# Pair 3 of batch 0 turned by transposing transfers, centroid halves in two banks, wide tanh and gate in the first unit, and a new written order

## The chip, the cores and the metric

The kernel runs on one core of one Trainium2 chip. The metric is device time in microseconds, the median of several runs. The kernel before took 301.54 us (three runs, 300.48 to 303.38).

The core has five engines with a queue each, and they run side by side: PE multiplies matrices, DVE and ACT do elementwise work (ACT has exp and tanh), POOL does simple elementwise work, and SP issues transfers. An engine takes its instructions strictly in the order in which they were written. An instruction whose inputs are not ready holds up everything behind it on its engine.

## The reference, cut to what matters

Clustered attention for 4 batches, 8 heads, 768 positions and head size 64, and behind it a two-layer network over the 3072 tokens.

```python
q_assign = argmax(einsum('bhsd,hcd->bhsc', q / |q|, c / |c|))   # 16 centroids per head
k_assign = argmax(einsum('bhsd,hcd->bhsc', k / |k|, c / |c|))
mask     = q_assign[:, :, :, None] == k_assign[:, :, None, :]
scores   = where(mask, q @ k.T / 8, -1e9)
attn     = exp(scores - max) / sum(exp(scores - max))
x        = (attn @ v) as [3072, 512]
h        = x @ w_in                 # 512 -> 2048
out      = (h * sigmoid(h)) @ w_out # 2048 -> 512
```

The argmax has to be right for nearly every position, so the products with the centroids need more than 16 bits. The kernel splits q and k into a high and a low float16 part.

## The kernel before, in words

**Tiles.** A batch has 8 heads in 4 pairs (pair p holds heads 2p and 2p+1). A head has 6 tiles of 128 positions for k and 6 for q. Each pair has a buffer `ab` in SBUF in which every tile lies turned: 64 rows of the high part and, in rows 64 to 95, a one-hot code of the tile's cluster, scaled so that the product of two different codes drives the exponent to zero. Scores are then one product of 96 rows (L685), with the mask in it.

**Steps.** `build` makes a graph of steps, each with the engines that may do it. Names in this document are those tags. For a part of batch b, pair p, head h, from tile t they are `p{b}.{p}.{h}.{t}` with a letter:

- `t` turns the tiles, `hi` and `lo` make the two parts, `v` moves half of the high part to the lower rows
- `l` multiplies with the centroids (logits), `m`, `b`, `o`, `f` find the largest, subtract it, make the one-hot code and flip it in blocks of 32
- `c` puts the code into `ab`, four copies of 32 rows, each by POOL, DVE, ACT or as a transfer on SP

Attention steps are `a{b}.{head}.{first q tile}`: `S` scores (L685), `E` exp (L688), `V` product with v (L713), `R` and `N` reciprocal and normalisation, `X` the turn of the result (L770) and `Y` its copy. Units of the network are `m{b}.{first tile}`: `U` up (L801), `T` tanh (L809), `G` gate (L812), `D` down (L828), `L` copy out, `O` store. Loads are `ld{b}.{p}` (q, k) and `lv{b}.{p}` (v), `cv` the cast of v; `win`, `wout` load weights and `cin`, `cout` cast them.

**Two ways to turn a part.** `part2` (L562 on, used for the first 8 tiles of each head of batch 0: 6 of k, 2 of q) turns two float32 tiles at once on PE (L579, four transposes per head), makes `hi` and `lo` out of PSUM and then moves half of `hi` with `v`. Its logits are three products for each pair of tiles (L624 to L626), with centroids that lie in `st2`. For pairs marked "22" the two heads share one round of `m`, `b`, `o`, `f`; pair 0, marked "2", has one round for each head. `part` (L465 on) splits the tiles as they lie in SBUF and turns both parts together with one transposing transfer on SP (L517), and its logits are products with `stk` (L529, L530 in batch 0, L532 later). All other parts go this way: q tiles 2 to 5 of batch 0 (`p0.p.0.8`) and batches 1 to 3.

**Stages.** Batch 0 goes in three rounds of two q tiles ([0,2), [2,4), [4,6)) so that the first unit of the network, `m0.0` (tokens of q tiles 0 and 1, all 8 heads), can start early. `m0.0` has 256 columns. Its 16 `U` steps are 4 matmuls of 256 columns each, its 16 tanh and 16 gates are 256 wide. The other units are `m0.2` with 512 columns and two of 384 in each later batch.

**Order.** The order on every engine is written out by hand: `PLAN` is a packed list of (step, engine) in order and of buffer numbers. It also holds dummy products with zeros (L951), 43 of 256 columns, in places where PE would wait. There are 8 PSUM banks; each `S`, `U`, `D`, turn and logit step takes one.

**The centroids** (L307 to L361) are loaded on ACT's queue, normalised (`csq` on DVE, `croot` on POOL, `csplit` on DVE), turned by one transpose of [128 x 128] into one bank (`cturn`, L330), and copied: `cplace2` into `st2` (two steps of two copies, one on ACT, one on DVE), and `cplace` into `stk` (three copies on DVE).

Of the kernel before, what the change touches and what calls it, by code (L numbers as in the profile page):

```python
# [12 lines left out]
f32 = mybir.dt.float32  # L13
f16 = mybir.dt.float16
AF = mybir.ActivationFunctionType
ALU = mybir.AluOpType
# [9 lines left out]
    "11543XvaUa;<08X8W*vvspm({+9jHIiazwtnnkkNf5nk&?iyp>(J@a+%_i5zs8%TrcSts4^|Y{weeZ43*}M&!mD2no=3a?r4yn=N*jx(y&wjafjU"
    "2n;uFckmvp8&K5U|(Bnke-4Enr6k{oPB=#GuV_$L?p)?s33mRMbRk*w&duya{%9ll)m~1~F!Tyo^$=#F{*HO&)q#=*7O59YGrf@%A}!W>11<7t+|"
    "7hD_`@X7{wSAv4m;rJxy~Xe&*?+||p$h<Uc+E@<W*WAfg$^(Ee9jl=W8rs~AlxJb4!lW5*2Y<65#Bdx6_VY7Q)#JT3WsM&>(jlGD8&sg(s*UZ<;f"
    "{@u&=b=3b{Ld~%Y_C_jV{Dwbe)c(bH&W|()aGDnop<~^5BT*t*3Z@l8Jb$H!)8yy_IXiTQ<LoZkYM&M?2nDo<L!UMRP2DMJTd02bY<%E!)67&EOt"
    "zO25c4a)+lP{=o-~ZCfMp6XXmW=k1;Fe%`3@N)u4IPklBl{t%TmXI(|gQnf&y2FWzLeYi1iV@t<1rBmUF8=#84l4%=u?G^2uk74z~zRX3eoy@*+*"  # L30
# [957 lines left out]
```

## Time and profile before

| | |
|---|---|
| median of three runs | 301.54 us |
| the profiled execution's own time | 301.66 us |
| its span, first to last instruction | 299.9 us |
| granted TensorE clock | 0.998 |
| busy: PE, DVE, ACT, POOL | 291.2, 213.9, 222.6, 89.6 us |
| first scores, first exp | 12.22, 13.50 us |
| first `U` of the first unit, its first tanh | 38.7, 39.77 us |
| first `U` of the second unit | 59.9 us |
| last matmul starts | 296.6 us |

Times inside a run count from the span's start. The profiled execution's own time is 1.8 us longer than its span. Matmuls overlap, so their listed durations are longer than their share of PE; how fast PE goes is read from how far apart their starts lie.

### The profile page before, as it was taken

What the parts mean: (1) busy time and instruction counts of PE and PEld (TensorE: products, weight loads), DVE (VectorE), ACT (ScalarE), POOL (GpSimd) and SP (SyncE); (2) the same over time, 40 slices, a digit from 0 to 9 for tenths busy, and PEclk for the clock granted to TensorE, in tenths of its full rate; (3) what the DMA queues carried; (4) which work ended last, traced back from release to release, by engine and by line L of the source; (5) the groups of instructions that cost most, each with busy time, mean ns of one, the idle gap of its engine ahead of it and who ended that gap; (6) DMA issues with size and microseconds to landing.
All of it is one profiled execution on the core that took longest, in us unless ns stands there. A gap on an engine that the chain in (4) does not pass through costs nothing.

```text
span 299.9 us, 7820 instructions
## 1 busy us (share of the span) xinstructions
PE 291.2 (97%) x3044; PEld 187.0 (62%) x3044; DVE 213.9 (71%) x512; ACT 222.6 (74%) x456; POOL 89.6 (30%) x151
## 2 busy tenths in 40 slices
PE   7898999999999999999999999999999999999995
PEld 5776898645555676766656566566665655554553
DVE  5999988878898999889999686676552323465140
ACT  2898999888669898998888867889988732343221
POOL 3787776443655406040833212100200000000000
PEclk9999999999999999999999999999999999999999
DMA  7899999498999999899485688500201111021022
GB/s 203 263 227 291 218 262 348 116 281 293 249 283 243 232 245 215 224 202 300 124 170 126 134 144 196 149 5 3 66 2 26 28 32 67 0 93 49 1 107 105
DMA packets 83382, 47.42 MB, mean 158 GB/s; under 512 B 60688, under 2 KB 78352, under 8 KB 83344
## 3 DMA queue, kind: packets, MB, share of 16 engines
q1 hardware_dynamic: 83200, 46.88, 63.6%
q8 instruction: 24, 0.39, 0.6%
q14 instruction: 14, 0.11, 0.1%
q10 hardware_dynamic: 144, 0.03, 0.1%
HBM read 27.30 MB, written 6.29 MB: 112 GB/s over the span
## 4 chain that ended last, share of the span: by engine, by line
PE 83%; DVE 10%; ACT 2%; issue 2%; DMA 1%; POOL 1%; SPq 0%; DVEq 0%
PE M L801 26%; PE M L828 26%; PE M L685 17%; PE M L713 10%; DVE hl L459 3%; PE M L532 2%; DMA nat<-in_q_dram 1%; DVE gq L812 1%; DVE lo L599 1%; DVE ab L191 1%; DVE ohT L436 1%; POOL ab L191 1%; DVE oh L429 1%; DVE mx L419 1%; DVE M L422 1%
## 5 line engine op out<-in xcount | busy, mean ns | idle before, releaser
L688 ACT ACTIVATE P<-M 128x512 f16<-128x512 f32 x288 | 155.8, 622 | 18.6 <-PE M L685 17.9
L812 DVE SCALAR_TENSOR_TENSOR gq<-tn,M 128x384 f16<-128x384 f32 (+2 forms) x128 | 66.7, 548 | 47.9 <-ACT tn L809 46.4
L801 PE MATMUL M<-xt,win_s 128*128 128x384 f16 (+2 forms) x512 | 95.7, 325 | 0.0
L828 PE MATMUL M<-wout_s,gq 128*128 128x512 f16 (+2 forms) x400 | 94.8, 370 | 0.0
L685 PE MATMUL M<-ab 96*128 96x256 f16 (+1 forms) x432 | 90.5, 308 | 1.4 <-DVE ab L191 0.9
L809 ACT ACTIVATE tn<-M 128x384 f32<-128x384 f32 (+2 forms) x128 | 61.2, 512 | 36.5 <-PE M L801 32.4
L801 PEld LDWEIGHTS <-win_s 128*128 128x128 f16 x512 | 48.7, 97 | 33.5 <-issue 0.2
L828 PEld LDWEIGHTS <-gq 128*128 128x128 f16 x400 | 37.4, 97 | 36.2 <-issue 0.4
L191 POOL COPY ab<-ohT 32x384 f16<-32x384 f16 (+2 forms) x69 | 38.4, 557 | 55.6 <-DVE ohT L436 31.2
L713 PEld LDWEIGHTS <-P 128*128 128x128 f16 x1152 | 45.7, 97 | 10.5 <-issue 0.7
L713 PE MATMUL M<-vt,P 128*128 128x65 f16 x1152 | 49.2, 193 | 0.3 <-DVE oh L429 0.2
L685 PEld LDWEIGHTS <-ab 96*128 96x128 f16 x432 | 38.0, 97 | 18.3 <-DVE ab L191 0.7
L459 DVE SCALAR_TENSOR_TENSOR hl<-nat,hl 128x768 f16<-128x768 f32 (+1 forms) x28 | 29.6, 1073 | 0.1
L191 POOL CAST vt<-nv 128x384 f16<-128x384 f32 x19 | 11.3, 607 | 32.5 <-DMA nv<-in_v_dram 21.3
L456 POOL TENSOR_SCALAR hl<-nat 128x768 f16<-128x768 f32 (+1 forms) x19 | 15.1, 804 | 19.4 <-DMA nat<-in_k_dram 14.2
L436 DVE STREAM_TRANSPOSE ohT<-oh 128x384 f16<-128x384 f16 (+2 forms) x33 | 18.3, 557 | 1.0
L401 DVE TENSOR_REDUCE M<-M 128x192 f32<-128x384 f32 x24 | 13.4, 559 | 6.1 <-PE M L532 4.4
L189 ACT COPY ot<-M 128x512 f32<-128x512 f32 (+2 forms) x14 | 7.8, 558 | 12.0 <-PE M L828 12.0
L191 DVE COPY ot<-M 128x512 f32<-128x512 f32 x11 | 7.6, 687 | 8.9 <-PE M L828 8.9
L429 DVE TENSOR_SCALAR oh<-M 128x96 f16<-128x96 f32 (+4 forms) x62 | 13.1, 252 | 0.7
L743 DVE TENSOR_TENSOR xn<-M,rz 128x384 f16<-128x384 f32 x24 | 13.1, 551 | 0.7 <-DVE rz L732 0.3
L732 DVE RECIPROCAL rz<-M 128x6 f32<-128x6 f32 (+1 forms) x36 | 6.6, 182 | 8.3 <-PE M L713 8.1
(60 smaller groups left out, 174.6 us busy)
## 6 DMA issues: line engine op xcount, KB each, us to landing
nv<-in_v_dram SPq DMA_DIRECT2D x16, 384.0 KB, 5.1
out_dram<-ot SPq DMA_DIRECT2D x23, 256.0 KB, 2.5
nat<-in_k_dram SPq DMA_DIRECT2D x15, 384.0 KB, 4.7
...
```

Source lines behind the costliest of these rows:

```text
L191: eng(en).tensor_copy(out, in_)
L429: e.nc.vector.tensor_scalar(out=T(oh)[:, 0:n, 0:HC].rearrange("p (g i) c -> p g i c", g=groups)[:, :, i0:i1, :], in0=from_().rearrange("p ...
L436: e.nc.vector.transpose(T(ohT)[:, 0:n, :].rearrange("p n c -> p (n c)"), T(oh)[:, 0:n, :].rearrange("p n c -> p (n c)"))
L456: e.nc.gpsimd.tensor_scalar(out=dh(), in0=src(), scalar1=QS, scalar2=1.0, op0=ALU.mult, op1=ALU.mult)
L459: e.nc.vector.scalar_tensor_tensor(out=dl(), in0=src(), scalar=QS, in1=dh(), op0=ALU.mult, op1=ALU.subtract)
L685: e.nc.tensor.matmul(bank(sb)[:, at : at + 128 * (c - a)], ab[0:96, kt[m], :], q, start=True, stop=True)
L688: e.nc.scalar.activation(out=T(P)[:, 0:n], in_=bank(sb)[:, 0:n], func=AF.Exp, bias=0.0, scale=ESC)
L713: e.nc.tensor.matmul(bank(O)[:, at : at + D + 1], T(P)[:, c : c + 128], T(vb)[:, VW * m : VW * m + D + 1], start=(m == 0), stop=(m == NJ - ...
L801: e.nc.tensor.matmul(bank(bk)[:, 0:n], e.win_s[:, r, ts(fb, 128)], T(X)[:, r, 128 * j0 : 128 * j1], start=(r == 0), stop=(r == NR - 1),)
L809: e.nc.scalar.activation(out=T(tn)[:, 0:n], in_=bank(bk)[:, 0:n], func=AF.Tanh, bias=0.0, scale=1.0)
L812: e.nc.vector.scalar_tensor_tensor(out=gq(fb // 4)[:, fb % 4, 0:n], in0=T(tn)[:, 0:n], scalar=1.0, in1=bank(bk)[:, 0:n], op0=ALU.add, op1= ...
L828: e.nc.tensor.matmul(bank(bk)[:, 0 : c1 - c0], gq(quarter)[:, fc % 4, ts(t, 128)], e.wout_s[:, fc, c0:c1], start=(fc == 0), stop=(fc == NF ...
```

## The change

1. **Pair 3 of batch 0.** `FIRST` for pair 3 goes from "22" to "DMA": its first 8 tiles of each head go through `part`. Two steps `hi`, two steps `lo` of 8 tiles read SBUF, two transposing transfers turn them, logits are 16 tiles x 2 products with `stk`, and each head has its own `m`, `b`, `o`, `f`. The four `v` and `t` steps of this pair and its `lo2` are gone.
2. **Centroids.** The two halves are turned by two transposes into two banks. `cplace2` now copies heads 0 and 1 alone (two small copies per half), `cplace3` the other six heads. Pair 0's logits wait for `cplace2`, pairs 1 and 2 for `cplace3`. `cplace` waits for both.
3. **The first unit.** With n = 256 columns, two `U` steps share a bank, and one tanh and one gate of 512 columns serve both: 8 of each in place of 16. `D` steps wait for the wide gates. Units of 384 and 512 columns are as before.
4. **Sizes.** 21 buffers `P` for 19; `mx`, `oh`, `ohT` hold 16 tiles in place of 24; `half` is placed earlier; `EARLY` (empty) is gone.
5. **The order** is new on every engine, with 57 dummy products in place of 43.

```diff
-FIRST = ["2", "22", "22", "22"]
+FIRST = ["2","22","22","DMA"]
...
-    "P": (19, [128, 512], f16),
+    "P": (21, [128, 512], f16),
...
-    pc = buf("M", 64)
+    pcs = [buf("M", 64), buf("M", 64)]
...
-        e.nc.tensor.transpose(bank16(pc)[:, 0:128], e.chl.rearrange("p a d -> p (a d)"), e.ident)
+        for part, pc in enumerate(pcs):
+            e.nc.tensor.transpose(bank16(pc)[0:64, 0:128], e.chl[:, part, :], e.ident)
...
+    s_pair = [
+        step("DVE ACT", c_place2(part, 0, 2), after=[s, s_const2], use=[pcs[part]], kind="place2", size=300, tag="cplace2")
+        for part in range(2)
     ]
-    s_cent = step("DVE", c_place, after=[s, s_const, s_cent2], use=[pc], kind="const", size=690, tag="cplace")
+    s_others = [
+        step("DVE ACT", c_place2(part, 2, H), after=[s, s_pair[part]], use=[pcs[part]], kind="place2", size=430, tag="cplace3")
+        for part in range(2)
+    ]
+    s_cent = step("DVE", c_place, after=[s, s_const, s_others], use=pcs, kind="const", size=690, tag="cplace")
...
-        s_log = step("PE", logits, after=[s_hi, s_lo, s_cent2], use=[A, lo2, Lb], kind="mm", size=(3 * w, 32), tag=tag + "l", key=key + 1)
+        s_log = step("PE", logits, after=[s_hi, s_lo, s_others if p else s_pair], use=[A, lo2, Lb], kind="mm", size=(3 * w, 32), tag=tag + "l", key=key + 1)
...
+        per = 512 // n if n <= 256 else 1
+        for f0 in range(0, NFB, per):
+            bk, tn = buf("M", n * per), buf("tn")
...
+            for fb in range(f0, f0 + per):
...
+                ups.append(
+                    step("PE", up, after=[xs, w_done["in"][fb // 2], ups], use=[bk, X], kind="mm", size=(NR, n), tag=tag + "U", key=key + fb)
+                )
...
+            y = step("ACT", tanh, after=ups, use=[bk, tn], kind="T", size=n * per, tag=tag + "T", key=key + f0)
+            s = step("DVE", gate, after=[ups, y], use=[bk, tn, g4], kind="G", size=n * per, tag=tag + "G", key=key + f0)
+            gates.extend([s] * per)
```

The first steps of the order, read out of the packed list ("24 x" is a count of dummies; a number behind # tells repeated steps of one name apart; of a pair's loads, #0 is k, #1 the first two q tiles, the last one q tiles 2 to 5, and for pair 0 k comes in two, #0 for head 0 and #2 for head 1, with q at #1 and #3):

```
SP before   ld0.0#0 ld0.0#1 ld0.0#3 ld0.0#2 ld0.3#1 ld0.3#0 ld0.2#2 ld0.1#0 ld0.1#1 p0.0.0.8t ld0.2#1 ld0.2#0 lv0.3 lv0.0 ld0.1#2 p0.2.0.8t
SP after    ld0.3#1 ld0.3#0 ld0.0#1 ld0.0#0 ld0.0#3 ld0.0#2 lv0.3 ld0.1#1 p0.3.1.0t ld0.2#2 p0.3.0.0t ld0.1#0 ld0.2#1 p0.0.0.8t ld0.2#0 ld0.1#2

PE before   14x p0.0.0.0t 2x cturn 3x p0.0.1.0t 2x p0.0.0.0l 3x p0.3.1.0t p0.0.1.0l p0.3.0.0t 8x p0.1.1.0t p0.1.0.0t p0.0.0.8l a0.0.0S
PE after    24x p0.0.0.0t cturn 6x p0.0.1.0t p0.0.0.0l 8x p0.0.1.0l 9x a0.0.0S a0.0.0S a0.0.0S p0.3.0.0l p0.3.1.0l 2x p0.1.0.0t p0.1.1.0t a0.1.0S

ACT before  p0.0.0.0hi cplace2 p0.0.1.0hi p0.3.1.0hi p0.3.0.0hi c c c c p0.1.1.0hi p0.1.0.0hi E E E E p0.2.0.0hi p0.2.1.0hi E ...
ACT after   p0.3.1.0hi p0.0.0.0hi cplace2 cplace2 p0.0.1.0hi cplace3 cv0.3 p0.0.1.0v cplace3 c c E E E c p0.1.0.0hi p0.1.1.0hi E p0.1.1.0v E E p0.2.1.0hi E E p0.2.0.0hi E ...

DVE before  csplit p0.0.0.8hi cplace2 p0.0.0.0lo p0.0.0.8lo p0.0.0.0m p0.0.1.0lo b o (p0.0.1.0: m b) f ...
DVE after   csplit p0.3.1.0lo p0.3.0.0lo p0.0.0.8hi p0.0.0.0lo p0.0.0.8lo p0.0.0.0m b p0.0.1.0lo o f ...
```

Ahead of the first tanh ACT has 49 exps before and 50 after; ahead of the first `U` PE has 51 `S` steps, 12 `V`, 6 `X`, 12 logit steps and 8 turns before, and 50, 14, 5, 12 and 6 after.

More of the change, by code (lines that the diff above doesn't have):

```diff
@@ L26 @@
[L26 to L30, printed above, removed]
@@ L91 @@
 PAIRED = 6
-EARLY = {}
 CHUNK = 8
@@ L106 @@
     "xn": (3, [128, 6, 128], f16),
-    "mx": (3, [128, 24], f32),
-    "oh": (2, [128, 24, 32], f16),
-    "ohT": (2, [128, 24, 32], f16),
+    "mx": (3, [128, 16], f32),
+    "oh": (2, [128, 16, 32], f16),
+    "ohT": (2, [128, 16, 32], f16),
     "tn": (3, [128, 512], f32),
@@ L355, in build @@
     s = step("POOL", c_root, after=[s, s_ident], kind="const", size=520, tag="croot")
-    s = step("DVE", c_split, after=[s], kind="const", size=870, tag="csplit")
-    s = step("PE", c_turn, after=[s, s_ident], use=[pc], kind="mm", size=(1, 128), tag="cturn")
-    s_cent2 = [
-        step("DVE ACT", c_place2(part), after=[s, s_const2], use=[pc], kind="place2", size=2, tag="cplace2") for part in range(2)
-    ]
-    s_cent = step("DVE", c_place, after=[s, s_const, s_cent2], use=[pc], kind="const", size=690, tag="cplace")
+    s = step("DVE", c_split, after=[s], kind="const", size=950, tag="csplit")
+    s = step("PE", c_turn, after=[s, s_ident], use=pcs, kind="mm", size=(2, 128), tag="cturn")
+    s_pair = [
+        step("DVE ACT", c_place2(part, 0, 2), after=[s, s_const2], use=[pcs[part]], kind="place2", size=300, tag="cplace2")
+        for part in range(2)
+    ]
+    s_others = [
[3 more added lines that the diff above has]
+    s_cent = step("DVE", c_place, after=[s, s_const, s_others], use=pcs, kind="const", size=690, tag="cplace")
     abuf, ready = {}, {}
@@ L801, in up @@
                         e.nc.tensor.matmul(
[L802 to L806 removed]
+                            bank(bk)[:, c0 : c0 + n], e.win_s[:, r, ts(fb, 128)], T(X)[:, r, 128 * j0 : 128 * j1],
@@ L812, in gate @@
+            def gate(_, f0=f0, bk=bk, tn=tn):
                 e.nc.vector.scalar_tensor_tensor(
-                    out=gq(fb // 4)[:, fb % 4, 0:n], in0=T(tn)[:, 0:n], scalar=1.0, in1=bank(bk)[:, 0:n],
-                    op0=ALU.add, op1=ALU.mult,
-                )
-            y = step("ACT", tanh, after=[s], use=[bk, tn], kind="T", size=n, tag=tag + "T", key=key + fb)
-            gates.append(step("DVE", gate, after=[s, y], use=[bk, tn, g4], kind="G", size=n, tag=tag + "G", key=key + fb))
+                    out=gq(f0 // 4)[:, f0 % 4 : f0 % 4 + per, 0:n], in0=T(tn)[:, 0 : n * per].rearrange("p (f c) -> p f c", c=n),
+                    scalar=1.0, in1=bank(bk)[:, 0 : n * per].rearrange("p (f c) -> p f c", c=n), op0=ALU.add, op1=ALU.mult,
+                )
@@ L926 @@
     e.wout_s = const.tile([128, NFB, DM], f16, name="wout_s")
+    e.half = const.tile([128, 1], f32, name="half")
     e.ident = const.tile([128, 128], f16, name="ident")
```

144 lines of the change are left out of this document (68 added, 76 removed).

## The prediction

> **What bounds the kernel now.** I read the page's busy times first, then busy time in four stretches, the chain of waits, and then the engines' own time lines up to 40 us.
>
> ```profile
> span 299.9 us, 7820 instructions
> PE 291.2 (97%) x3044; PEld 187.0 (62%) x3044; DVE 213.9 (71%) x512; ACT 222.6 (74%) x456; POOL 89.6 (30%) x151
> ```
> ```profile
> 0.00:12.20 12.20, 10.17 (x97) 8.07 (x98) 8.54 (x31) 5.50 (x11) 5.08 (x26) 1.00 0.75 209
> 12.20:38.60 26.40, 23.65 (x414) 20.37 (x412) 25.45 (x71) 25.28 (x52) 20.95 (x35) 1.00 1.07 259
> 38.60:59.90 21.30, 20.73 (x294) 17.40 (x292) 17.90 (x51) 20.46 (x49) 13.80 (x18) 1.00 0.87 237
> 59.90:296.60 236.70, 236.47 (x2248) 141.14 (x2246) 161.98 (x362) 170.88 (x346) 49.75 (x74) 1.00 0.57 137
> ```
> ```profile
> 38.74 1.36 PE M L801 x12
> ...
> 41.27 0.73 PE M L713 x24
> ...
> 45.19 0.66 PE M L685 x6
> ```
>
> The second number of the stretches is their length, then come busy PE, weight loads, DVE, ACT, POOL. From 38.60 on PE is busy 257.2 of 258.0 us. So the end is set by two things: when PE becomes dense, and how much PE work is then left. The chain shows 38.74 as the start of the first `U`. Nothing after that can be won but some 0.8 us of idle PE and work taken off PE itself. From 12.2 to 38.6 it is different: ACT is busy 25.28 and DVE 25.45 of 26.40, PE 23.65 with dummies in it. There the exps on ACT and the codes on DVE meter the work out to PE. So for the change I ask how far PE has come in its work when the units of the network begin.
>
> **The change part by part.**
>
> *PE's own work.*
>
> ```profile
> 7.92 0.18 PE L624 MATMUL M<-st,ab 128*128 128x32 f16 x1
> ...
> 7.95 0.18 PE L625 MATMUL M<-st,ab 128*128 128x32 f16 x1
> ...
> 10.90 1.04 PE L579 MATMUL M<-ident,nat 128*128 128x128 f32 x8
> ```
>
> Eight float32 turns of pair 3 go: eight took 1.04 us to the end of the last, which I put at 0.11 each from start to start, 0.87. Small products start 0.03 apart (7.92, 7.95; a little under, since both are rounded): 24 go and 32 come, +0.2, and one more centroid turn, +0.07. Together PE has 0.6 us less to do. The dummies lie where PE would wait, before and after, so I take 14 more at nothing; the cover is the wait itself, and if a wait behind a dummy were gone, the ten small ones after the first scores would cost 0.11 each, 1.1 us, which is within the range.
>
> *The first scores.*
>
> ```profile
> 1.05 3.17 PE L951 MATMUL M<-zeros 128*128 128x256 f16 x14 [1.05 <-DVE zeros L196]
> ...
> 4.02 1.06 PE L579 MATMUL M<-ident,nat 128*128 128x128 f32 x4
> ```
> ```profile
> DMA packets 830, 0.65 MB, mean 130 GB/s; under 512 B 188, under 2 KB 830, under 8 KB 830
> ```
> ```profile
> DMA packets 288, 0.40 MB, mean 333 GB/s; under 512 B 13, under 2 KB 288, under 8 KB 288
> ```
> ```profile
> 5.14 0.28 DVE L323 SCALAR_TENSOR_TENSOR chl<-tn,ci,chl 128x64 f16<-128x64 f32 x1
> 5.90 0.84 DVE L454 TENSOR_SCALAR hl<-nat 128x512 f16<-128x512 f32 x1 [0.48 <-DMA nat<-in_q_dram]
> ...
> 7.13 0.69 DVE L599 SCALAR_TENSOR_TENSOR lo<-M,ab 128x512 f16<-128x512 f32 x1
> 7.74 0.68 DVE L459 SCALAR_TENSOR_TENSOR hl<-nat,hl 128x512 f16<-128x512 f32 x1
> 8.35 0.29 DVE L419 TENSOR_REDUCE mx<-M 128x8 f32<-128x128 f32 x1
> ...
> 10.29 0.43 DVE L436 STREAM_TRANSPOSE ohT<-oh 128x256 f16<-128x256 f16 x1
> ```
> ```profile
> 10.85 1.65 ACT L189 COPY ab<-ohT 32x256 f16<-32x256 f16 x4
> 12.53 1.08 ACT L594 ACTIVATE ab<-M 128x512 f16<-128x512 f32 x2
> 13.50 2.09 ACT L688 ACTIVATE P<-M 128x512 f16<-128x512 f32 x4
> 15.47 1.09 ACT L594 ACTIVATE ab<-M 128x512 f16<-128x512 f32 x2
> 16.43 12.04 ACT L688 ACTIVATE P<-M 128x512 f16<-128x512 f32 x24
> 29.30 3.54 ACT L688 ACTIVATE P<-M 128x512 f16<-128x512 f32 x7 [0.83 <-PE M L685]
> 33.09 6.96 ACT L688 ACTIVATE P<-M 128x512 f16<-128x512 f32 x14 [0.25 <-PE M L685]
> 39.77 0.55 ACT L809 ACTIVATE tn<-M 128x256 f32<-128x256 f32 x1
> 40.04 0.78 ACT L688 ACTIVATE P<-M 128x512 f16<-128x512 f32 x1
> ```
>
> The loads of pair 3 (0.13 + 0.39 MB) now stand ahead of pair 0's. Pair 0's first k and q end after 0.85 MB in place of 0.33. In the first 5 us 0.65 MB had moved (the first of the two packet rows, window 0 to 5 us); later the queue gives 0.40 MB in 1.2 us (the second, 12.4 to 13.6). So they land near 5.6 us, and the first turn starts there and not at 4.02. The 24 dummies fill this: 14 took 3.17 us, 0.22 each, so at that pace they'd end at 6.3, and at 5.6 if they speed up at 5 us as the turns do (four in 1.06 at 4.02, eight in 1.04 at 10.90).
>
> The lateness is hidden by DVE. After `csplit` (5.14 + 0.28) DVE now has two `lo` of pair 3, 0.6 each by the distance of 7.13 and 7.74, then p0.0.0.8hi (0.84, or less without its wait), and starts p0.0.0.0lo near 7.5 to 7.8, where it was 7.13. From there the order on DVE is nearly as before (8.35 is the first peak, 10.29 the flip): with one `lo` earlier in between I get the flip at 10.3 to 10.7. Two puts each on POOL and ACT follow, 0.41 apiece by the ACT row, where ACT had three in a row; scores at 11.8 to 12.1 for 12.22. The two `cplace2` on ACT (0.5 apiece at most) end near 7.9, in time for that `lo`. Then the gain: before, two `hi` of pair 1 stood ahead of the first exp (12.53, exp at 13.50). Now the exp comes first, 0.45 behind its scores: 12.25, that is 1.25 earlier.
>
> *ACT up to the first tanh.* Among the exps now stand one exp more (0.49), two `hi` more (0.97 by 12.53 to 13.50), one put (0.41) and p0.1.1.0v, a copy of [64 x 512].
>
> ```profile
> L191 POOL COPY ab<-ab 64x512 f16<-64x512 f16 x8 | 5.7, 727 | 3.6 <-ACT ab L594 3.4
> ```
>
> This copy ACT has not done before; it lies between its put of 256 columns, 0.41, and POOL's 0.73 for the same copy. I take 0.55. Sum +2.4 - 1.25 = +1.2. Idle ACT was 0.83 + 0.25 in this stretch, and I leave it at 1.1 to 1.2: it comes in other places, below. So the first tanh moves from 39.8 to 41.0 by ACT.
>
> DVE as a second count, from the first flip to the last copy of round [0,2): three `hi` come to DVE (+1.7 by 0.84 for one of 512 and less for the others), two `lo` have gone ahead of it (-1.2), codes of pair 3 go by head (+0.6), the codes of head 1 fall behind the flip (+0.6), three wide puts and one copy less (-1.3): +0.4. Between +0.4 and +1.2 I take +0.85, nearer to ACT, whose rows cover more of it.
>
> *The queue of SP.* Behind p0.3.1.0t and p0.3.0.0t, which wait for their `lo` (6.1 and 6.7), stand ld0.2#2, ld0.1#0, ld0.2#1, p0.0.0.8t and ld0.2#0. Pair 1's turns on PE wait for ld0.1#0, and with them ACT's two `hi` and every exp behind them.
>
> ```profile
> DMA packets 1091, 0.28 MB, mean 165 GB/s; under 512 B 1056, under 2 KB 1091, under 8 KB 1091
> ...
> ab<-hl SPq DMA_TRANSPOSE x1, 3.2
> ```
>
> The one transfer of this size (8 tiles, 0.26 MB; window 9.6 to 11.3) ran at 165 GB/s, 1.6 us of the queue, and landed 3.2 us after its issue. The loads ahead are 1.84 MB: at 333 GB/s from 5 us on they end at 8.6. Two such transfers (3.2), ld0.2#2 (0.8) and ld0.1#0 (1.2) then end at 13.8, usable near 14.1. ACT wants its first `hi` of pair 1 after three exps and a put, at 14.1 too, and the turn lies between: 0.5 us of idle ACT. For pair 2, ld0.2#0 ends at 17.0, and the same count leaves 0.2. With 0.5 for a late put later on that is the 1.2 of above.
> [...]
>
> *The wide tanh and gate.*
>
> ```profile
> L809 ACT ACTIVATE tn<-M 128x512 f32<-128x512 f32 x16 | 9.1, 600 | 4.3 <-PE M L801 3.4 <-DVE gq L812 0.5 <-ACT P L688 0.3
> ```
>
> A tanh of 256 holds ACT 0.27 (39.77 to 40.04). One of 512 lasts 0.60, and the exps of 512 follow each other at 0.50 (12.04 for 24). Eight at 0.50 for sixteen at 0.27 save 0.3 us; the gates save some of DVE's time, which isn't full there. Between 38.6 and 59.9 PE lacks 0.57, and ACT is the full one (20.46 of 21.30), so I credit 0.3.
> [...]
>
> *The rest.* The larger `P` pool and the smaller tiles cost nothing, and no row shows `S` waiting for a `P`. The order after 60 us is new too: PE is idle for 0.23 there now, so it can hardly gain, and I take 0, with 1 us of loss as its other end. The tail is the same: two narrow pieces, a copy, a store.
>
> *Sum.* The `U` steps begin 0.85 later; PE has then done 0.25 us less (one `S` of 0.22, one `X` and two turns of 0.44 less, two `V` of 0.37 and 0.2 of logits more), and has 0.6 less in all, so 0.35 less to do: +0.85 - 0.35 - 0.3 = +0.2. The profiled execution took 301.66, so 301.9; the median of the runs stands 0.1 below it: 301.7.
>
> **The rivals.**
>
> *PE dense from 20 us on (faster).* Pair 3's exps are at hand before pair 1's codes, and could fill the gaps that PE has today.
>
> ```profile
> 24.59 0.60 PE L685 MATMUL M<-ab 96*128 96x256 f16 x4 [0.27 <-DVE ab L191]
> ...
> 28.65 1.05 PE L685 MATMUL M<-ab 96*128 96x256 f16 x8 [0.64 <-DVE ab L191]
> ```
>
> For it: these gaps wait for DVE's puts of pairs 1 and 2, idle PE from 12.2 to 38.6 is 2.75 us, and the 11 dummies that the order has there (0.11 each, 1.2 us) hide more. Were nearly all of it gone, with the rest of the sum: 301.7 - 3.5 = 298.2. Against it: ACT and DVE are full in that stretch, and both get more to do.
>
> *SP's queue late (slower).* If each transposing transfer holds the queue until it lands, 3.2 us in place of 1.6, ld0.1#0 comes at 17.3, ACT and PE stand behind p0.1.0.0t, and the end moves by that: 301.7 + 3.2 = 304.9. It decides from 14.1 on: each us by which pair 1's k is later costs one. For it: the one such transfer started at an idle queue, so how it runs behind loads isn't shown. Against it: loads issued behind it moved data right after it.
>
> *Transfers as fast as loads.* At 333 GB/s each of the two takes 0.8, so the loads come 1.6 earlier and ACT's 0.7 of waiting for them goes: 301.0. The 165 GB/s speak against it. [...]
>
> *The change doesn't do what it says:* the wide tanh serves only 256-column units, so it can do no more than the 0.3; this is in the forecast.
>
> **How the numbers follow.** A change of under 1%, 3 us, can't be told from none; the three runs before spread by 2.9. Forecast 0.55, transfers as loads 0.07, dense PE 0.18, SP late 0.20. Faster by over 1%: 0.18 (298.2 is 1.1% below). Slower by over 1%: 0.20. Same: 0.62. Range: down to 298.0, where the dense rival lies, and up to 305.0, which takes in the slow one and the unknown late order.
>
> **What would show it.** Right: the first exp near 12.3, the first tanh near 41, the first `U` near 39.5, PE busy in all but 1 us from there, and DMA transposes at about 165 GB/s. Pair 1's turns at 14 to 15 us show the queue; at 17 the slow rival holds. PE idle under 1 us between 13 and 38 would be the dense rival. Wrong in any case if the distance from the first `U` to the last matmul isn't 257 to 259 us.

## The result, and the profile after

The changed kernel took 305.49 us (median of six runs), the kernel before 301.72 us beside it. The ratio is 1.0103, with a 95% interval of 1.0068 to 1.0137: the change is slower, and whether by more than the 1% that parts the prediction's classes can't be told. Two of the six runs (309.77 and 310.98) were in a slower state and don't count in the ratio; the other four have a median of 304.96. The prediction was 301.7 us, with a range of 298.0 to 305.0, so that median lies at its upper edge. The profiled execution took 305.32 us.

The page after (busy time), and then the busy time in the stretches that the prediction used: length, PE, weight loads, DVE, ACT, POOL, granted clock, DMA share, GB/s.

```profile
span 303.5 us, 7878 instructions
PE 292.9 (96%) x3059; PEld 188.0 (62%) x3059; DVE 206.7 (68%) x496; ACT 230.7 (76%) x466; POOL 83.0 (27%) x148
```
```profile
0.00:12.20 12.20, 9.45 (x81) 7.08 (x81) 7.99 (x27) 6.35 (x16) 4.57 (x25) 1.00 0.93 218
12.20:38.60 26.40, 23.81 (x407) 20.65 (x408) 23.27 (x69) 23.26 (x48) 18.06 (x33) 0.94 1.05 249
38.60:59.90 21.30, 21.30 (x318) 18.44 (x317) 17.25 (x47) 21.23 (x44) 13.90 (x19) 1.00 0.98 261
59.90:300.00 240.10, 237.98 (x2255) 141.61 (x2253) 157.86 (x354) 179.44 (x361) 46.46 (x71) 1.00 0.57 136
```

Two rows are worse than before. In the first, PE is less busy than it was (10.17). In the last it lacks 2.12 us, where it lacked 0.23. From 38.6 to 59.9 it is full now, where it lacked 0.57: the dense stretch comes as the prediction had it, and is worth about that much.

The lines of the engines' time line for the milestones (start, length, engine, line, what it does; in brackets the wait before it):

```profile
5.48 0.30 PE L581 MATMUL M<-ident,nat 128*128 128x128 f32 x1
6.79 0.55 PE L581 MATMUL M<-ident,nat 128*128 128x128 f32 x3 [1.01 <-DMA nat<-in_k_dram]
...
12.71 1.08 ACT L690 ACTIVATE P<-M 128x512 f16<-128x512 f32 x2 [0.56 <-PE M L687]
...
13.96 0.27 PE L581 MATMUL M<-ident,nat 128*128 128x128 f32 x1
...
41.45 0.60 PE L803 MATMUL M<-xt,win_s 128*128 128x256 f16 x4
```

These are the first product of pair 0's turn, on its q tiles (4.02 before), its other three, on k, the first exp (13.50 before), the first product of pair 1's turn, on q as well, and the first `U` (38.74 in the chain of before, 38.63 on PE's own line). Pair 1's k followed at 14.64. The first tanh started at 42.97 (39.77 before). The waits of PE from 5 to 25 us, of ACT from 12 to 41, and of PE from 100 to 122 (engine, line, releaser: us in all, how often, the longest):

```profile
PE M L531 <- DMA ab<-hl: 1.5, 1, 1.5
PE M L581 <- DMA nat<-in_k_dram: 1.4, 2, 1.0
...
ACT P L690 <- PE M L687: 1.6, 2, 1.0
ACT ab L596 <- PE M L581: 1.6, 3, 0.7
...
PE M L687 <- DVE M L403: 2.1, 1, 2.1
```

**The start.** L531 is p0.0.0.8l, the logits of pair 0's later q tiles. It waits for its transposing transfer, and everything behind it on PE waits too. The chain of waits has that transfer at 11.77 with 5.65 us to landing; the same transfer in the kernel before took 3.2.

```profile
11.77 5.65 DMA ab<-hl
17.43 0.05 issue
17.48 0.18 PE M L531
```

Why it took so long is seen in the transfers from 13.9 to 17.4 us (GB/s in 40 slices, and the one packet of PE's own instructions in that stretch):

```profile
GB/s 281 307 328 304 290 281 249 401 219 164 105 249 266 266 281 97 18 3 0 0 0 0 3 9 6 9 9 12 9 9 9 53 402 357 369 474 351 88 140 369
...
q8 instruction: 1, 0.02, 2.5%
```

For 1.3 us, from 15.3 to 16.6, the core's DMA engines moved next to nothing (6 GB/s in the mean); such a stretch is called a standstill below. A packet with 16 KB of PE's instructions was on its way from 14.52 to 15.92, and the 256-byte packets of the transposing transfer, of which half take 0.018 us or less, took up to 1.48.

**The clock.** Behind that wait the granted clock (the third number from the right) fell:

```profile
16.00:18.00 2.00, 0.53 (x17) 0.52 (x18) 0.89 (x2) 1.28 (x3) 1.69 (x5) 1.00 0.76 227
18.00:20.00 2.00, 2.00 (x25) 1.77 (x22) 1.83 (x5) 1.31 (x3) 0.00 (x0) 0.59 1.07 363
20.00:22.00 2.00, 2.00 (x22) 1.76 (x21) 1.77 (x5) 1.35 (x3) 1.70 (x4) 0.55 1.21 318
```

From 18.4 to 21.8 us the clock was at half (0.50 over these 3.4 us). Twelve large products and a dummy ran there at half pace, 0.213 apart for 0.108, some 0.105 us more each, 1.4 us in all; the small ones kept their distance of 0.027. PE was busy for 1.9 of the 3.4 us ahead of the fall, and for 1.3 of the 3.4 us from 115.25 on, where no fall followed, so an idle PE alone didn't decide it. Of the experiments' profiles that are read below only e11_start_only shows such a fall, and that at 94 us, so it isn't in every execution.

**The middle.** The other 2.1 us lie at 116 us. The engines' time line from 114 on (SPq is SP issuing a transfer):

```profile
112.78 1.48 SPq L519 DMA_TRANSPOSE ab<-hl  x1
...
115.47 2.10 SPq L762 DMA_TRANSPOSE xt<-xn  x1
...
117.47 0.56 DVE L456 TENSOR_SCALAR hl<-nat 128x768 f16<-128x768 f32 x1 [2.90 <-DMA nat<-in_q_dram]
117.94 0.56 DVE L403 TENSOR_REDUCE M<-M 128x192 f32<-128x384 f32 x1
```

DVE stands 2.9 us at p2.3.1.0hi, for the load ld2.3#1. Behind it stands the sum L403 that frees a PSUM bank, and PE wants that bank. The load was issued at 112.10, 2.5 us before DVE came to that step; in the kernel before SP issued it at 98.97, and DVE came to the step at 108.29. And again 16 KB of PE's instructions came (115.47), and the longest packet of the transposing transfer took 2.13 us.

**A ledger for PE.** For every matmul I take the distance to the next one's start, less the usual distance of its kind (the tenth percentile of its shape); dummies count whole. The sum is what PE didn't spend on the kernel's own work at its usual pace, in us by stretch:

| | 0-15 | 15-20 | 20-60 | 60-100 | 100-150 | behind | sum | last matmul ends |
|---|---|---|---|---|---|---|---|---|
| before | 8.28 | 1.40 | 5.58 | 1.00 | 0.76 | 1.32 | 18.34 | 296.80 |
| after | 10.47 | 2.61 | 4.48 | 0.63 | 2.92 | 1.77 | 22.86 | 300.35 |

The rest is the kernel's own work: 278.5 before, 277.5 after. So the end moved by 4.5 - 1.0 = +3.5: 2.2 were lost up to 15 us, 1.2 up to 20, 2.2 from 100 to 150 and 0.4 behind, and 1.1 + 0.4 were won between 20 and 100. Counted again with kinds told apart by the printed shapes, the sums come out within 0.25 us and the work saved at 0.6, so differences of 0.4 us in this ledger mean little.

### The profile page after: what moved, and what is told of

Same layout as the page of the kernel before. It is cut to its first block, busy times and chain, and to the rows that moved or that the text cites. A ratio compares the mean times of both kernels' runs of the same rounds, so it can differ in the third digit from the quotient of the medians.

```text
span 303.5 us, 7878 instructions
## 1 busy us (share of the span) xinstructions
PE 292.9 (96%) x3059; PEld 188.0 (62%) x3059; DVE 206.7 (68%) x496; ACT 230.7 (76%) x466; POOL 83.0 (27%) x148
## 4 chain that ended last, share of the span: by engine, by line
PE 84%; DMA 6%; ACT 5%; DVE 2%; SPq 1%; issue 1%; DVEq 0%; ACTq 0%
PE M L803 26%; PE M L833 25%; PE M L687 18%; PE M L715 11%; ACT P L690 3%; PE M L534 2%; DMA ab<-hl 2%; DMA nat<-in_q_dram 2%; DMA nat<-in_k_dram 1%; DMA gq<-in_moe_w_out_dram 1%; PE M L581 1%; PE M L772 1%; SPq L239 0%; SPq L762 0%; DVE lo L601 0%
## 5 line engine op out<-in xcount | busy, mean ns | idle before, releaser
L690 ACT ACTIVATE P<-M 128x512 f16<-128x512 f32 x288 | 153.9, 633 | 18.3 <-PE M L687 17.4
L687 PE MATMUL M<-ab 96*128 96x256 f16 (+1 forms) x432 | 91.8, 309 | 2.8 <-DVE M L403 2.1
L816 DVE SCALAR_TENSOR_TENSOR gq<-tn,M 128x384 f16<-128x384 f32 (+1 forms) x120 | 65.7, 574 | 37.3 <-ACT tn L813 36.6
L813 ACT ACTIVATE tn<-M 128x384 f32<-128x384 f32 (+1 forms) x120 | 59.5, 527 | 30.1 <-PE M L803 28.2
L190 POOL COPY ab<-ohT 32x384 f16<-32x384 f16 (+2 forms) x80 | 43.5, 544 | 97.4 <-DVE ohT L438 44.3
L687 PEld LDWEIGHTS <-ab 96*128 96x128 f16 x432 | 38.5, 98 | 18.9 <-issue 0.8
L461 DVE SCALAR_TENSOR_TENSOR hl<-nat,hl 128x768 f16<-128x768 f32 (+1 forms) x30 | 27.8, 934 | 1.6 <-ACT hl L454 1.1
L403 DVE TENSOR_REDUCE M<-M 128x192 f32<-128x384 f32 x24 | 13.6, 565 | 11.3 <-PE M L534 8.5
L190 DVE COPY ot<-M 128x512 f32<-128x512 f32 (+1 forms) x14 | 9.2, 660 | 15.1 <-PE M L833 15.0
L458 POOL TENSOR_SCALAR hl<-nat 128x768 f16<-128x768 f32 (+1 forms) x18 | 14.3, 794 | 17.6 <-DMA nat<-in_q_dram 8.2
L188 ACT COPY ot<-M 128x512 f32<-128x512 f32 (+1 forms) x11 | 6.4, 579 | 13.4 <-PE M L833 13.3
L190 POOL CAST vt<-nv 128x384 f16<-128x384 f32 x16 | 10.2, 650 | 16.3 <-DMA nv<-in_v_dram 15.9
L431 DVE TENSOR_SCALAR oh<-M 128x96 f16<-128x96 f32 (+2 forms) x64 | 13.5, 250 | 0.7
```

Source lines behind the costliest of these rows:

```text
L190: eng(en).tensor_copy(out, in_)
L403: e.nc.vector.tensor_reduce(out=bank(dst)[:, at : at + HC * n].rearrange("p (n c) -> p n c", c=HC), in_=bank(src)[:, 0 : 32 * n].rearrange ...
L458: e.nc.gpsimd.tensor_scalar(out=dh(), in0=src(), scalar1=QS, scalar2=1.0, op0=ALU.mult, op1=ALU.mult)
L461: e.nc.vector.scalar_tensor_tensor(out=dl(), in0=src(), scalar=QS, in1=dh(), op0=ALU.mult, op1=ALU.subtract)
L687: e.nc.tensor.matmul(bank(sb)[:, at : at + 128 * (c - a)], ab[0:96, kt[m], :], q, start=True, stop=True)
L690: e.nc.scalar.activation(out=T(P)[:, 0:n], in_=bank(sb)[:, 0:n], func=AF.Exp, bias=0.0, scale=ESC)
```

## The experiments

Each ratio is to the kernel before, run beside it. Where only the order is edited, the diff shows the steps of an engine in order. Lines of `S` and turns move by two in these kernels (L685, L579, L529 or L532 for L687, L581, L531 or L534).

### Does the stalled transfer at 15 us cost, and how

```diff
 PE  (e1_wide_dummies)
-24 products with zeros of 256 columns, then p0.0.0.0t ...
+12 products with zeros of 512 columns, then p0.0.0.0t ...
 PE  (e2_fill)
-a0.1.0S#0, 1 dummy, p0.0.0.8l
+a0.1.0S#0, 13 dummies, p0.0.0.8l
 PE  (e4_late_8l; the codes of p0.0.0.8 follow on DVE, behind p0.1.1.0lo, and p0.2.1.0hi and a put wait with them)
-p0.0.0.8l, a0.1.0S#2, a0.1.0S#1, p0.1.0.0l, p0.2.1.0t, a0.6.0S#2, a0.6.0S#1
+a0.1.0S#2, a0.1.0S#1, p0.1.0.0l, a0.6.0S#2, a0.6.0S#1, p0.0.0.8l, p0.2.1.0t
```

> The changed kernel with its first 24 dummy products of 256 columns written as 12 of 512 columns (the zeros tile is widened for it): the same time on PE, but 24 PE instructions fewer, so that PE's later 16 KB instruction transfers fall 12 matmuls later in its order. Collision theory: the transfer p0.0.0.8t took so long because the 16 KB instruction packet (14.52 us, 1.40 us long) fell into it; with the packet later, p0.0.0.8l starts near 16.0 and not at 17.48, PE's idle 1.52 us there is under 0.4, the clock stays whole from 18 to 22 us, the first tanh comes at 41 or earlier (42.97), and the kernel is 2 to 3 us faster than the changed one: ratio to the kernel before 1.000 to 1.004. Full-queue theory: three transposing transfers and the loads between them simply take that long; p0.0.0.8l still starts at 17 or later, ratio 1.008 to 1.014. The later instruction packets shift too, so the 2.2 us gap at 116 us may go or stay.

> The changed kernel with 13 dummy products in place of 1 ahead of p0.0.0.8l, where PE idles 1.52 us: 12 x 0.11 = 1.3 us of filling. It prices the halved clock by itself (granted 0.59 and 0.55 at 18 to 20 and 20 to 22 us): if the clock falls because PE stood idle, it stays whole here, the 16 matmuls that ran at half pace (0.105 us each) run at full, and the first U comes up to 1.7 us earlier than 41.45; ratio to before about 1.005. If ACT and DVE set the pace there anyway, the clock costs nothing: first tanh still near 43, ratio about 1.010.

> The changed kernel with p0.0.0.8l moved behind a0.1.0S, p0.1.0.0l and a0.6.0S on PE (1.2 us of PE work), its codes behind p0.1.1.0lo on DVE, and p0.2.1.0hi behind two exps on ACT. It takes away what PE waits behind, not the late transfer. If the late transfer hurts only because it stands ahead of ready work, PE idles under 0.6 us from 15 to 19 us, the clock stays whole, and the kernel is 1.5 to 3 us faster than the changed one: ratio 1.000 to 1.005. If everything in that stretch is late together (loads of pair 2 behind the same transfer), PE waits for p0.2.1.0t instead, and the ratio stays at 1.008 to 1.011.

Measured: 1.0102 (1.0066 to 1.0138), 1.0079 (1.0052 to 1.0107), 1.0184 (1.0101 to 1.0268). Twelve products fewer moved the instructions' packet from 14.52 to 14.88 us only, too little to part it from the transfer's wake: PE still waited 1.6 us for it. The first run by itself so leaves its question open. Three later profiles help: in e6_shift, e8_phase and e10_all no such packet falls into that transfer, and it landed after 3.94, 4.64 and 4.43 us. In the other nine of this start it took 4.42 to 6.42, with a median of 5.65. So, as far as these few show, a full queue takes it from 3.2 to some 4.3, and the packet, mostly, to 5.65.

With the dummies of e2_fill the granted clock stayed at 1.00, and the first `U` came 1.0 us earlier (40.45). Their ratio lies between the two forecasts (1.005 and 1.010), 0.0024 below the change's, well within the intervals. What the dip costs is better seen in the mean granted clock that is on record for each run: 3.4 us at half clock take 0.006 off it. Of the 78 runs of the kernel before that were taken beside the experiments, 18 show 0.994 or less, and they are 0.9 to 1.6 us longer in the mean than the others of their set. Two of the change's four runs show it (305.49 for 304.15 us in the mean), and none of e2_fill's ten. So a run with the dip, and with the wait ahead of it, is some 1.3 us longer; but the dip occurs in the kernel before as well. To let other work pass the late logits (e4_late_8l) made it no better, and the runs of that kernel scatter most.

### Does the gap at 116 us belong to DVE's order

```diff
 DVE  (e3_late_hi)
-p2.3.1.0hi, p2.1.1.0L, p2.3.1.0lo, p2.1.1.0m, b, o
+p2.1.1.0L, p2.1.1.0m, b, o, p2.3.1.0hi, p2.3.1.0lo
```

> The changed kernel with p2.3.1.0hi and lo moved behind p2.1.1.0L, m, b and o on DVE; nothing else. In the changed kernel DVE stood 2.9 us before that hi (116 us) waiting for its load, p2.1.1.0L stood behind it, and PE stood 2.07 us before a score step whose bank that L had to free. If that is the whole chain, the gap goes and the end comes 2.0 to 2.2 us earlier: ratio 1.003 to 1.004. If PE only meets the next late thing (pair 3 of batch 2 is turned later now, its codes come later), less than 0.7 us is won: ratio 1.008 to 1.010.

Measured: 1.0112 (1.0059 to 1.0164). PE's busy time from 100 to 120 us, and its waits there and from 12 to 25:

```profile
100.00:120.00 20.00, 17.77 (x257) 11.71 (x256) 14.02 (x34) 16.05 (x31) 5.95 (x12) 1.00 1.09 188
```
```profile
PE M L532 <- DMA ab<-hl: 1.5, 1, 1.5
PE M L685 <- DVE xn L743: 0.7, 1, 0.7
...
PE M L529 <- DMA ab<-hl: 0.3, 1, 0.3
```

The bank of L403 is no longer waited for, but PE stands 2.2 us as it did (17.93 busy in after), now behind a transposing transfer and behind DVE's `xn`, which comes late because DVE still stands 1.8 us for the load of p2.3.1.0hi ahead of it. The second theory, the next late thing, is right, though its ratio lies just above the forecast. The transfers of 113 to 117 us show the same standstill, 1.7 us long, with a packet of instructions in it:

```profile
GB/s 333 302 302 294 256 251 197 184 151 108 61 26 41 179 0 0 0 0 0 0 0 0 0 8 8 8 10 10 10 8 20 261 289 287 287 292 292 292 292 321
...
q8 instruction: 1, 0.02, 1.5%
```

This profile also holds a start without the stall: p0.0.0.8l waited 0.3 us in place of 1.5. Its first exp and first `U`:

```profile
12.25 1.08 ACT L688 ACTIVATE P<-M 128x512 f16<-128x512 f32 x2 [0.56 <-PE M L685]
...
39.22 0.60 PE L801 MATMUL M<-xt,win_s 128*128 128x256 f16 x4
```

The prediction had 12.25 and 39.5. The first tanh started at 40.75, for 41.0.

### The late loads, and the phase of PE's instructions

```diff
 SP   (e5_early_loads)
-ld2.1#1, p2.0.0.0t, ..., m0.0O#0, ld2.2#0, p2.1.0.0t, ..., ld2.2#1, a1.3.0X, ld2.3#0, p2.1.1.0t, 2 puts, a1.1.0X, ld2.3#1, p2.2.0.0t, lv2.0
+ld2.1#1, ld2.2#0, ld2.2#1, p2.0.0.0t, ..., m0.0O#0, ld2.3#1, p2.1.0.0t, ..., a1.3.0X, p2.1.1.0t, ld2.3#0, p2.2.0.0t, 2 puts, a1.1.0X, lv2.0
 DVE
-p2.1.0.0L ... f, p2.2.0.0hi, ..., p2.2.0.0lo, ..., p2.0.1.0L ... f, p2.3.1.0hi, p2.1.1.0L, p2.3.1.0lo
+p2.2.0.0hi, p2.1.0.0L ... f, p2.2.0.0lo, ..., p2.3.1.0hi, p2.0.1.0L ... f, p2.3.1.0lo, p2.1.1.0L
 PE   (e8_phase, the change's order)
-24 products with zeros of 256 columns, then p0.0.0.0t ...
+96 products with zeros of 64 columns, then p0.0.0.0t ...
 PE   (e6_shift = e5_early_loads and)
-24, 6, 8 and 9 dummies of 256 columns
+12, 3, 4 and 5 dummies of 512 columns
```

> The order of after with one edit, between 89 and 116 us: on SP the loads ld2.2#0, ld2.2#1 go ahead of p2.0.0.0t, ld2.3#1 ahead of p2.1.0.0t, and p2.2.0.0t goes ahead of two puts, a1.1.0X and lv2.0; on DVE p2.2.0.0hi and lo and p2.3.1.0hi go some 4 us earlier. Theory A (the new order issues the loads and turns of batch 2's pairs 2 and 3 too late: ld2.3#1 at 112.1 us, 98.97 before; p2.2.0.0t at 112.8, 103.9 before): PE's loss between 100 and 120 us falls from 2.5 us to 0.6 or less, and the ratio to before from 1.010 to 1.003-1.004. Theory B (a transposing transfer stands still for 1.5 to 2.5 us whenever PE's 16 KB of instructions come while it runs, and PE soon waits for whatever stands behind it, wherever it is put in the order): the loss stays at 2 us or more, ratio 1.008-1.011.

> The order of after, with the first 24 dummies of 256 columns in 96 of 64 columns: the same PE time, 72 matmuls more, so that every later 16 KB of PE's instructions (128 matmuls each) come a little over half a period earlier. Theory B (stall by PE's instructions): the transfers of 105.6 and 115.5 us come some 5 us earlier, the stall of 2.1 us at 115.1 is gone, and PE's loss between 100 and 120 us falls from 2.5 to 1 us or less, unless a new place collides too; ratio 1.002-1.006. Theory A (late loads and turns in the order): the loss stays at 2 us or more, ratio 1.009-1.011.

> e5_early_loads, and the first four groups of dummies in half as many products of 512 columns (26 matmuls fewer for the same time), so that PE's 16 KB of instructions come some 2 us later at the start than the 14.5 us of after, behind p0.0.0.8t. Theory: the stall of that transfer is what moves the first U from the forecast 39.5 to 41.45 in after's profile; then the first U comes at 39.2 to 39.8, and the ratio is 0.002 to 0.005 lower than that of e5_early_loads, 0.998-1.002 if that one is at 1.003. Rival: the start is late because ACT and DVE have more to do ahead of the first tanh, stall or none; then the ratio is that of e5_early_loads within 0.002.

Measured: 1.0059 (1.0037 to 1.0082), 1.0061 (1.0038 to 1.0084), 1.0081 (1.0050 to 1.0111). The rows from 100 to 120 us, of e5_early_loads first, then e8_phase, then e6_shift:

```profile
100.00:120.00 20.00, 19.62 (x267) 12.85 (x266) 15.94 (x40) 17.71 (x35) 9.52 (x16) 1.00 1.12 193
```
```profile
100.00:120.00 20.00, 18.93 (x262) 12.26 (x260) 14.82 (x36) 17.12 (x33) 7.23 (x13) 1.00 1.09 205
```
```profile
100.00:120.00 20.00, 19.89 (x271) 13.10 (x269) 16.23 (x39) 17.72 (x35) 9.47 (x15) 1.00 1.05 185
```

Either edit takes a good part of the gap: earlier loads 1.7 of 2.07 us, another phase of the instructions, with not a step of the order moved, 1.0. (By the ledger, in which the expectations count, the loss from 100 to 120 us falls from 2.5 to 1.0 and to 1.9: both fall short of their forecasts.) By the ratios each is worth some 0.004, 1.3 us, with intervals that still overlap the change's; part of that may be the clock, whose dip none of e8_phase's seven runs shows, two of e5_early_loads' eight, and two of the change's four. So the gap very likely has two parents: an order that has its loads only 2.5 us ahead of their use, and standstills that fall there. Neither theory holds alone. That they don't add up, e6_shift shows (PE full to 0.11 us here, first `U` at 39.26 as its theory wanted, and yet 1.0081, with 0.8 us of idle PE from 120 to 150 us), and so does the next pair.

### An earlier first `U`

```diff
 PE   (e9_scores_first = e5_early_loads and)
-p0.0.0.8l, a0.1.0S#2, a0.1.0S#1, p0.1.0.0l
+a0.1.0S#2, a0.1.0S#1, p0.1.0.0l, p0.0.0.8l
 DVE
-p0.0.0.8m, b, o, p0.1.1.0lo
+p0.1.1.0lo, p0.0.0.8m, b, o
 ACT to POOL (e10_all = e9_scores_first with the dummies of e8_phase and)
-p0.1.1.0v on ACT
+p0.1.1.0v on POOL
```

> e5_early_loads, and at the start p0.0.0.8l, which waits for its transposing transfer until 17 us in all profiles of this order but one, goes behind the two scores a0.1.0S#2 and #1 and behind p0.1.0.0l on PE; on DVE p0.1.1.0lo goes ahead of p0.0.0.8m. Theory (PE stands in order behind that transfer, ACT with it: 1.2 us from 16.87 to 18.04 in e5_early_loads): ACT's wait goes, the first U comes 0.8 to 1.2 us earlier than the 40.65 of e5_early_loads, and the ratio falls from 1.006 to 1.002-1.004. Rival (ACT waits a little later instead, for the codes that come out of p0.0.0.8l): first U within 0.3 us of 40.65, ratio 1.005-1.007.

> e9_scores_first with the 96 narrow dummies of e8_phase, and the copy p0.1.1.0v (0.61 us) on POOL instead of ACT. By the count of ACT in the prediction that copy costs the end its own length: first U 0.5 us earlier still, and with PE's loss of 0.98 us between 100 and 120 down to 0.5 or less the ratio is 0.998-1.001. Rival (ACT's time ahead of the first tanh is not what the end waits for): the ratio of e9_scores_first within 0.002.

Measured: 1.0072 (1.0043 to 1.0101) and 1.0101 (1.0056 to 1.0146). ACT's waits from 12 to 41 us in e5_early_loads, and then in e9_scores_first:

```profile
ACT P L688 <- PE M L685: 2.0, 3, 1.2
ACT ab L594 <- PE M L579: 0.4, 1, 0.4
```
```profile
ACT P L688 <- PE M L685: 0.8, 2, 0.6
ACT ab L594 <- PE M L579: 0.6, 1, 0.6
```

One us of ACT's wait went, and the first `U` came at 39.65 for 40.65, just as forecast. The time didn't follow. (Seven of the 14 runs of the kernel before beside it had the clock's dip, which flatters its ratio: without the runs that have it, on either side, e5_early_loads is at 1.0057 and e9_scores_first at 1.0095.) PE's rows from 100 to 140 us of e9_scores_first, where a standstill of 3.0 us falls at 115.4:

```profile
100.00:120.00 20.00, 19.90 (x269) 12.87 (x267) 16.33 (x40) 17.86 (x35) 8.84 (x14) 1.00 1.07 162
120.00:140.00 20.00, 19.11 (x162) 11.58 (x163) 16.18 (x36) 17.32 (x38) 6.58 (x10) 1.00 0.86 187
```

By the ledger PE lost 0.42 us from 60 to 100 and 1.58 from 100 to 150 in e5_early_loads, and 1.21 and 2.14 here: 1.35 more. The won microsecond is given back between 60 and 150 us. In e10_all neither forecast holds: the first `U` is at 40.60 again, since PE now stands for a code that comes as a transfer, and PE is idle for 1.42 us from 100 to 150. Its longest wait from 5 to 25 us, which e9_scores_first doesn't have:

```profile
PE M L685 <- DMA ab<-ohT: 1.2, 1, 1.2
```

### The wide tanh and gate undone

```diff
-                e.nc.scalar.activation(out=T(tn)[:, 0 : n * per], in_=bank(bk)[:, 0 : n * per], func=AF.Tanh, bias=0.0, scale=1.0)
+                for c in range(0, n * per, n):
+                    e.nc.scalar.activation(out=T(tn)[:, c : c + n], in_=bank(bk)[:, c : c + n], func=AF.Tanh, bias=0.0, scale=1.0)
```

and the gate in the same way.

> The order of after, with each wide tanh as two of 256 columns and each wide gate as two. Prediction's sum: 8 tanh of 0.50 for 16 of 0.27 save 0.3 us, so this is 0.3 us slower than after, ratio 1.011. Rival 1: ACT isn't what PE waits for between 41 and 60 us, so the same as after, 1.010. [...]

Measured: 1.0121 (1.0084 to 1.0159), against 1.0103 of the change: 0.5 us slower by the ratios, with intervals that overlap. The sign is the forecast's; between 0 and 0.3 us it doesn't decide.

### The change's start with the later order of before

```diff
-the whole order of the change
+the change's order for the first 660 common steps (e11_start_only) or 666 (e12_smooth_seam), then the order of before
```

> The changed kernel with its own order up to its 660th step that both kernels have (about 86 us: pair 3 by transposing transfers, the centroids, the loads, the wide tanh and gate are all in this stretch), and from there on the order and buffers of before. Theory 1 (the start of the change costs little or nothing, some 0.2 us by the ledger up to 100 us of e5_early_loads, and the order behind it loses the rest between 100 and 120 us): PE's loss between 100 and 120 us at 0.5 us or less, ratio 0.998-1.003. Theory 2 (the start is what costs, and the later wait is only where a PE that comes too soon gives it back): ratio 1.005-1.010, with the loss between 100 and 120 us at 1 us or more in this order too.

> Again the start of the changed kernel and the later order of before, joined with less harm: e11_start_only lost 4.5 us between 80 and 100 us, most of it right behind the seam (2.24 us at 90.8, PE behind a code of pair 3 of batch 1 whose turn had just been issued), which neither kernel has. Here the seam is at the 666th common step (about 87 us), heads 6 and 7 of batch 1 change places in the part from before, since the changed order turns head 6 first, and the P buffers behind the seam go by the one freed longest. Theory 1 (the change's start and wide tanh cost nothing to 1 us, and its later order loses the rest): loss between 80 and 120 us at 1.5 us or less (0.95 in before), ratio 0.998-1.003. Theory 2 (a PE that comes earlier or with another phase loses it there in any order): loss between 80 and 120 us at 2.5 us or more, ratio 1.006-1.010. Above 1.015 the seam itself decides again and the run tells neither.

Measured: 1.0349 (1.0304 to 1.0394) and 1.0084 (1.0053 to 1.0116). The first is spoiled by its seam: 2.3 us of PE idle between 80 and 100 us, and 2.9 behind 150, most of it where ACT waits 2.8 us for an `ot` buffer whose store isn't done. The second has a clean seam. Its rows of PE:

```profile
100.00:120.00 20.00, 19.91 (x289) 13.28 (x287) 16.70 (x43) 18.30 (x36) 7.47 (x12) 1.00 1.17 200
120.00:140.00 20.00, 18.77 (x173) 11.62 (x171) 17.33 (x41) 17.32 (x37) 3.78 (x7) 1.00 1.05 209
```

For comparison the kernel before, where this order is at home:

```profile
100.00:120.00 20.00, 20.00 (x291) 13.39 (x290) 18.76 (x47) 18.63 (x37) 8.29 (x13) 1.00 1.08 232
120.00:140.00 20.00, 20.00 (x194) 12.87 (x193) 17.64 (x41) 18.78 (x41) 3.29 (x6) 1.00 1.00 226
```

Up to 120 us theory 1 holds, 0.9 us of ledger loss from 80 to 120. But then, from 120 to 150, 2.3 us of idle PE come that before doesn't have, and the ratio is theory 2's; as written, neither theory holds. The change's later order isn't the only one that loses there: the order of before loses too, behind this start. Some of that may be due to the two heads that change places and to the buffers, which behind the seam often have the numbers of neither kernel (`P` above all, but PSUM banks too); this wasn't tried apart.

### All of them side by side

| | ratio | first `U` | PE idle 100-150 | ledger 0-15 | ledger 0-60 | sum of ledger |
|---|---|---|---|---|---|---|
| before | 1 | 38.63 | 0.00 | 8.28 | 15.3 | 18.34 |
| after | 1.0103 | 41.45 | 2.07 | 10.47 | 17.6 | 22.86 |
| e1_wide_dummies | 1.0102 | 40.57 | 2.33 | 9.88 | 16.5 | 22.61 |
| e2_fill | 1.0079 | 40.45 | 2.22 | 10.39 | 16.4 | 22.47 |
| e3_late_hi | 1.0112 | 39.22 | 2.23 | 9.97 | 15.2 | 20.95 |
| e4_late_8l | 1.0184 | 40.44 | 2.80 | 9.86 | 16.4 | 22.49 |
| e5_early_loads | 1.0059 | 40.65 | 0.41 | 10.05 | 16.6 | 20.27 |
| e6_shift | 1.0081 | 39.26 | 0.88 | 9.87 | 15.2 | 19.89 |
| e8_phase | 1.0061 | 39.85 | 1.07 | 10.81 | 15.8 | 19.83 |
| e9_scores_first | 1.0072 | 39.65 | 0.99 | 9.73 | 15.9 | 20.98 |
| e10_all | 1.0101 | 40.60 | 1.42 | 10.60 | 16.8 | 21.08 |
| e12_smooth_seam | 1.0084 | 40.73 | 2.41 | 10.35 | 16.7 | 22.34 |

All but the ratios come from one execution each, the ratios from several; the ledger up to 60 us is the second count. No version beats the kernel before; the nearest are e5_early_loads and e8_phase. What all of them have in common is the first 15 us: 1.5 to 2.5 us more that PE doesn't work. Up to 60 us this is made up in full where p0.0.0.8l doesn't hold up PE (e3_late_hi, e6_shift: 15.2 for 15.3), and in the others in part or not at all.

## Why the prediction was right and wrong

**The range was met at its edge, and partly by luck.** It reached to 305.0 for a slow queue of SP, which didn't come as written, and for the unknown late order, which did. The sum itself was 3.4 us short for the profiled execution, 301.9 for 305.3, and in its own terms it comes apart like this: the first `U` was 2.0 later than forecast (41.45 for 39.5), and behind 60 us PE was idle 1.9 more than before, where 0 was taken; against that, the idle time between 38.6 and 59.9 went down by 0.57, 0.3 more than credited, and PE had 0.6 less to do behind the first `U`, 0.2 more than forecast (256.6 us busy for 257.2). 301.9 + 2.0 + 1.9 - 0.3 - 0.2 is 305.3.

**PE's own work: right.** Forecast -0.6, the ledger has -1.0, or -0.6 by the second count.

**The first scores and exp: nearly right.** The loads were put at 5.6 us. The q part was there at 5.48, the k part at 6.79 only (row above). First scores came at 12.29 for 11.8 to 12.1, the first exp at 12.71 for 12.25, and at 12.25 in e3_late_hi. DVE did hide the lateness from the scores.

**"The lateness is hidden by DVE" held for the scores, and not for PE's early work.** Before, PE turned pairs 3 and 1 and did p0.0.0.8l ahead of the first scores, while it waited; now it runs dummies until the loads come and does the turns of pair 1 behind the scores (13.96 for 10.90). The first scores are not later, but PE has done less by then: 9.45 us busy, with more dummies, for 10.17; 10.47 us of ledger loss up to 15 us for 8.28. By itself this doesn't move the end: e3_late_hi and e6_shift lose 9.96 and 9.87 there, and up to 60 us no more than before, since the dummies and waits behind 20 us leave room for what PE didn't do early. The prediction's way, to ask when the first `U` comes and how much PE has left then, wasn't at fault.

**The queue of SP is one of the two steps that failed: the right queue, the term too small.** Pair 1's k was turned from 14.64 on, near the forecast (14.1), so the slow rival as it was written, 17.3 with pair 1 standing, is refuted. But the 1.2 us that the sum gave ACT for all its waits became 3.2 (1.6 and 1.6), because a transfer that nobody in the sum waited for, p0.0.0.8t, took 5.65 us to landing. Where PE hardly stood for it (e3_late_hi, 1.4 us of ACT's wait), the first `U` came at 39.22 for the forecast 39.5; with the wait and a full clock, at 40.6 (e1_wide_dummies, e5_early_loads); with the dip behind it, at 41.45. So the count of ACT up to the first tanh was sound, and a transfer's time to landing behind other transfers, taken from one at an idle queue, wasn't. The prediction calls that one the only transfer of its size. The trace of before has two more of 8 tiles, issued at 14.07 and 21.37 among other transfers, and they show what was missing (us to landing, the last number):

```profile
ab<-hl SPq DMA_TRANSPOSE x1, 4.9
...
ab<-hl SPq DMA_TRANSPOSE x1, 6.0
```

**The wide tanh: not settled.** 0.3 us was credited; e7_narrow gives 0.5, with more than a us of uncertainty. What PE lacked from 38.6 to 59.9, 0.57 us, is gone.

**"The order after 60 us ... I take 0, with 1 us of loss as its other end" is the other step that failed.** PE was idle for 2.12 us there, 1.9 more than before. The argument was that PE was idle for only 0.23 us; this bounds the gain and not the loss. The trace of before had the rows for a warning: a standstill of 1.4 us, with 0.02 MB of instructions just ahead of it, hit the transfers there at 109 us, and PE had no wait by it.

```profile
GB/s 289 289 292 284 292 287 287 533 384 402 389 328 369 328 243 233 238 241 243 77 64 28 20 0 20 41 20 20 13 18 18 92 269 289 287 289 294 289 289 292
...
q8 instruction: 1, 0.02, 1.7%
```

(Transfers of the kernel before, 107 to 111 us; PE is busy for all of that stretch.)

**The dense rival (298.2)** failed by its own sign: PE is idle for 2.5 us between 13 and 38, where it asked for under 1. Only by the ledger, which counts dummies too, did PE lose 1.1 to 2.3 us less than before between 20 and 60 us, in every one of these profiles.

**Transfers as fast as loads (301.0)** had a point. The 165 GB/s aren't the pace of an undisturbed transfer. The second one of pair 3 went through from 11.26 to 12.20 us:

```profile
DMA packets 1075, 0.28 MB, mean 292 GB/s; under 512 B 1065, under 2 KB 1075, under 8 KB 1075
```

The loads had 333. The first one took 2.87 us (7.73 to 10.60), with a standstill of 1.16 in it. Together they held the queue for 3.8 us, where the forecast had 3.2 by the wrong pace, so that pair 1's k came near its time by luck. What slows such transfers here are the standstills, and the 301.0 had no place for them.

**The test "distance from the first `U` to the last matmul 257 to 259 us"** passed, 258.7, and told little: the forecast itself stood at 257.3 (258.0 before, less 0.35 and 0.3), and the test was wide enough to take in most of the 2.1 us of idle PE. e5_early_loads, nearer to the kernel before in time, fails it with 256.9.

**What stays open:** how the 0.6% that is left in e5_early_loads and e8_phase splits. By the second count e5_early_loads loses 1.2 us up to 60 us and 0.3 behind it, e8_phase 0.5 and 0.9, against 0.6 of work saved; but no run undid the loads' order or pair 3's transfers alone. And why the order of before, at its own place, meets such standstills without a wait is answered only by "its loads go out earlier"; e12_smooth_seam says that this isn't all.
